# A lighter float64-to-float32 conversion of the weights, with its first pass tied to the exponentials and the Relus

## The chip, the cores and the metric

The kernel runs on one NeuronCore of a Trainium2 chip. The metric is device time in microseconds (us), the median of several executions. The names of the engines are those of the profile: PE is TensorE (matmuls; PEld its weight loads), DVE is VectorE, ACT is ScalarE, POOL is GpSimd, SP is SyncE, which here only issues DMAs.

## The reference

Inputs: q, k, v of 8 batches x 8 heads x 576 positions x 64 in float32; U (576x32), V (32x576), w_ch1 (512x2048) and w_ch2 (2048x512) in float64.

```
scores = q k^T / 8, masked: heads 0-3 the last 32 positions, heads 4-7 positions with the same pos % 32
x  = softmax(scores) v                       # 8 x 576 x 512, heads side by side
u  = x + (x^T U V)^T                         # mixing over positions, rank 32
out = u + relu(u w_ch1) w_ch2                # float32
```

The result has float32 accuracy. Each float32 operand of a large product is therefore split into a high and a low part (hi + lo, in the matmul's reduced float32 format), and each product is done in three matmuls: hi hi, hi lo, lo hi.

## The kernel before

**The main loop.** The 4608 rows of u are cut into 18 blocks of 256. A step is one block and one of 16 slices of 128 of the hidden layer: `gemm1` (12 matmuls of 256 columns into the PSUM tile `ph`, which has two buffers), then on ACT the Relu `gh` (L629), on DVE the remainder `gl` (L630, which reads `ph` and so frees it), and two steps later `gemm2` (12 matmuls of 512 columns, two tiles of 6, into an accumulator). There are 288 steps. The first two blocks run interleaved, since every slice of the weights is converted while they run.

**The attention.** Batch 0 comes ahead of the first step, batch 1 partly beside the last part of batch 0 and partly beside the first steps, and the others in windows of later steps. Batches 0 and 1 do all heads on PE; from batch 2 on the strided heads are done with products on POOL and sums on DVE (`strided_heads`). In batches 0 and 1 a pair of heads goes through: transposes of k and q on PE (L203), copies on ACT (`kZ`, `qT`), scores (L299), maximum and subtraction on DVE (L322, L324), the exponential on ACT (L325), transposes (L330), the product with v (L340), the division (L367 to L369). The mixing follows (L475 to L509), and then u^T is built (`uh`, `ul`, L590 to L595).

**The conversion of the weights.** There are 32 chunks of 128x512 (`raw`, 64-bit), in four groups of 8, 4 for `gemm1` and 4 for `gemm2`. `to_f32` makes float32 of the 64-bit patterns:

- on ACT, the absolute value of the high words read as float32 (L115);
- the maximum of this and 2^-15 (L116), by `CMODE` on POOL in six chunks of eight and on DVE in two;
- on DVE, a shift left by 3 and a mask (L118), then sign and top exponent bit or-ed in from the high words (L120), then the top 3 bits of the low words (L122);
- afterwards in `weights`, on ACT the high part (L169), and on POOL the low part, a subtraction (L170).

The three small arrays (U and two pieces of V) go through the same `to_f32`, with the maximum on DVE. All of the conversion lies ahead of about 193 us.

**What sets the order.** Each engine runs its instructions in one queue, in order. A conversion is called from the first attention's loop (one chunk in five turns) and from the step loop (by `CONVM`, and at the latest when a step needs it). The order that results on each engine is not the order of the code: a scheduler with its own estimate of times moves instructions within what the data allows. `tc.issue_after(ins)` adds to an instruction the condition that it stands behind `ins` on the same engine; before, only the weights' DMAs use it.

Of the kernel before, what the change touches and what calls it, by code (L numbers as in the profile page):

```python
# [16 lines left out]
TINY = 2.0 ** -15  # L17
# [11 lines left out]
CMODE = (1, 1, 1, 0, 1, 1, 1, 0)  # L29
# [17 lines left out]
def fused_kernel(ctx, tc, q, k, v, U, V, w1_in, w2_in, masks, eye, out):  # L47
# [31 lines left out]
    def psx2():  # L79
        """Two PSUM banks; those of the output sums serve too before the first of them."""  # L80
# [10 lines left out]
    last_dma = [None]  # L91
# [14 lines left out]
    def to_f32(raw, p, n, eng=nc.vector, one=False):  # L106
        """float32 of float64 bits: the top 24 significant bits; below float32's range 0."""
# [4 lines left out]
        if one:  # L112
            eng.tensor_scalar(out=f, in0=hi_w.bitcast(F32), scalar1=TINY, scalar2=None, op0=ALU.abs_max)
        else:
            nc.scalar.activation(out=f, in_=hi_w.bitcast(F32), func=AF.Abs)  # L115
            eng.tensor_scalar(out=f, in0=f, scalar1=TINY, scalar2=None, op0=ALU.max)  # L116
        i = cv.bitcast(I32)[0:p, 0:n]
        nc.vector.tensor_scalar(out=i, in0=i, scalar1=3, scalar2=0x3FFFFFF8,  # L118
                                op0=ALU.logical_shift_left, op1=ALU.bitwise_and)
        nc.vector.scalar_tensor_tensor(out=i, in0=hi_w, scalar=-0x40000000, in1=i,  # L120
# [39 lines left out]
    def weights():  # L160
        for n, (i, g, t) in enumerate(chunks):
# [3 lines left out]
            f = to_f32(raws[i, g, t], 128, 512, *((nc.vector, False), (nc.gpsimd, False), (nc.vector, True), (nc.gpsimd, True))[CMODE[n % 8]])  # L165
# [32 lines left out]
    def transpose_natural(dsts, xn, strided, engines):  # L198
        """dst[d, position] per head of load_natural, the positions class by class when strided."""
# [35 lines left out]
    def acquire(names):  # L235
        """The first of these buffers that no other part of the program is filling or reading, when one is free."""
        while True:
            for name in names:
                if name not in held:
                    held[name] = True  # L240
                    return name
            yield

    def value_tiles():
        """Values of two heads, each in its half of the rows and of the columns; what stays is written once."""
# [6 lines left out]
    def attention_pair(b, pr, sd, od, last):  # L252
        """Two heads of a batch: 32 positions attend to themselves and to the 32 before, in the order of the
        positions (local heads) or class by class (strided heads)."""
# [70 lines left out]
        nc.scalar.activation(out=s_sb, in_=s_sb, func=AF.Exp, scale=0.125 if early else 1.0)  # L325
# [459 lines left out]
```

## Time and profile before

| | us |
|---|---|
| median of 3 runs | 1016.41 (1016.31 to 1018.74) |
| the profiled execution: its span, the only time that the page gives of it | 1016.9 |
| PE busy | 958.7 |
| DVE busy | 648.8 |
| POOL busy | 406.1 |
| ACT busy | 313.0 |

An engine's busy time says little on its own here. The program has a first part of some 90 us, in which batch 0's attention leaves PE idle for much of the time, a second part of about 100 us, in which the steps have begun and the conversion still runs, and a third part of more than 800 us in which PE is nearly always busy. What a change to the conversion is worth is to be read from the first two parts.

### The profile page before, as it was taken

What the parts mean: (1) busy time and instruction counts of PE and PEld (TensorE: products, weight loads), DVE (VectorE), ACT (ScalarE), POOL (GpSimd) and SP (SyncE); (2) the same over time, 40 slices, a digit from 0 to 9 for tenths busy, and PEclk for the clock granted to TensorE, in tenths of its full rate; (3) what the DMA queues carried; (4) which work ended last, traced back from release to release, by engine and by line L of the source; (5) the groups of instructions that cost most, each with busy time, mean ns of one, the idle gap of its engine ahead of it and who ended that gap; (6) DMA issues with size and microseconds to landing.
All of it is one profiled execution on the core that took longest, in us unless ns stands there. A gap on an engine that the chain in (4) does not pass through costs nothing.

```text
span 1016.9 us, 18249 instructions
## 1 busy us (share of the span) xinstructions
PE 958.7 (94%) x7164; PEld 832.6 (82%) x7164; DVE 648.8 (64%) x1184; ACT 313.0 (31%) x691; POOL 406.1 (40%) x397
## 2 busy tenths in 40 slices
PE   4576889999999999999999999999999999999997
PEld 2345678898898889978889888988898889999996
DVE  3567998979786868634768686968686864312121
ACT  6777545213311241111422133123321242111110
POOL 1324966965383429201447353735383410000000
PEclk9797999999999999999999999999999999999999
DMA  7865913042523250401252425052514200101000
GB/s 189 221 164 143 366 39 67 2 109 48 91 42 68 48 90 22 88 1 42 47 91 43 68 47 91 21 89 48 91 39 71 47 22 21 42 1 43 1 21 21
DMA packets 186094, 71.33 MB, mean 70 GB/s; under 512 B 148952, under 2 KB 177272, under 8 KB 186008
## 3 DMA queue, kind: packets, MB, share of 16 engines
q1 hardware_dynamic: 186008, 70.16, 32.4%
q8 instruction: 56, 0.92, 0.4%
q14 instruction: 30, 0.25, 0.1%
HBM read 51.64 MB, written 11.80 MB: 62 GB/s over the span
## 4 chain that ended last, share of the span: by engine, by line
PE 76%; DVE 7%; SPq 5%; POOL 4%; issue 3%; DMA 3%; ACT 2%; DVEq 0%; POOLq 0%; ACTq 0%
PE ph L625 35%; PE acc L642 33%; SPq L94 4%; POOL tmp L409 3%; PE px L299 2%; PE px L340 1%; DVE cv L120 1%; DVE st L439 1%; PE px L330 1%; POOL w L170 1%; SPq L157 1%; DVE cv L122 1%; PE px L475 1%; DMA raw<-in_moe_w_ch_dram 1%; PE px L501 1%
## 5 line engine op out<-in xcount | busy, mean ns | idle before, releaser
L625 PE MATMUL ph<-uh,w 128*128 128x256 f32 x2304 | 472.6, 286 | 8.1 <-DVE gl L630 7.3
L625 PEld LDWEIGHTS ph<-uh,w 128*128 128x128 f32 x2304 | 379.3, 190 | 29.4 <-DVE gl L630 11.9
L642 PE MATMUL acc<-w,gh 128*128 128x512 f32 x1088 | 341.5, 393 | 0.0
L625 PE MATMUL ph<-ul,w 128*128 128x256 f32 x1152 | 331.5, 288 | 1.6 <-DVE ul L595 1.6
L630 DVE SCALAR_TENSOR_TENSOR gl<-ph,gh 128x256 fp32r<-128x256 f32 x288 | 120.6, 419 | 244.9 <-ACT gh L629 243.5
L629 ACT ACTIVATE gh<-ph 128x256 fp32r<-128x256 f32 x288 | 110.3, 384 | 504.9 <-PE ph L625 452.8
L437 POOL TENSOR_TENSOR tmp<-st,s_st 128x448 f32<-128x448 f32 (+7 forms) x162 | 144.2, 912 | 237.2 <-DVE st L439 148.7
L625 PEld LDWEIGHTS ph<-ul,w 128*128 128x128 f32 x1152 | 217.3, 189 | 11.4 <-DVE ul L595 1.8
L642 PEld LDWEIGHTS acc<-w,gh 128*128 128x128 f32 x1088 | 194.3, 188 | 31.2 <-issue 2.2
L642 PE MATMUL acc<-w,gl 128*128 128x512 f32 x544 | 213.2, 392 | 0.2 <-DVE gl L630 0.2
L409 POOL TENSOR_TENSOR tmp<-st 128x576 f32<-128x576 f32 (+6 forms) x162 | 169.4, 1089 | 74.9 <-DMA st<-in_k_dram 29.2
L439 DVE TENSOR_REDUCE st<-tmp 128x64 f32<-128x64 f32 (+8 forms) x162 | 138.3, 873 | 4.4 <-POOL tmp L437 3.4
L642 PEld LDWEIGHTS acc<-w,gl 128*128 128x128 f32 x544 | 102.2, 188 | 19.3 <-issue 1.1
L411 DVE TENSOR_REDUCE s_st<-tmp 128x9 f32<-128x576 f32 (+6 forms) x162 | 87.8, 564 | 14.2 <-POOL tmp L409 13.6
L170 POOL TENSOR_TENSOR w<-cv,w 128x512 fp32r<-128x512 f32 x32 | 45.3, 1424 | 49.1 <-ACT w L169 46.9
L116 POOL TENSOR_SCALAR cv<-cv 128x512 f32<-128x512 f32 x24 | 40.0, 1670 | 42.2 <-ACT cv L115 36.8
L454 ACT COPY xg<-st 32x256 f32<-32x256 f32 x96 | 38.7, 404 | 37.3 <-DVE st L439 36.4
L299 PE MATMUL px<-kZ,qT 128*32 128x128 f32 x612 | 30.5, 303 | 8.5 <-ACT qT L226 8.4
L299 PEld LDWEIGHTS px<-kZ,qT 128*32 128x32 f32 x612 | 20.4, 120 | 18.3 <-ACT qT L226 9.9
L169 ACT CAST w<-cv 128x512 fp32r<-128x512 f32 x32 | 19.7, 618 | 44.0 <-DVE cv L122 37.4
L612 DVE TENSOR_TENSOR ul<-u,uh 128x1024 fp32r<-128x1024 f32 x15 | 21.9, 1460 | 14.3 <-ACT uh L611 14.3
L120 DVE SCALAR_TENSOR_TENSOR cv<-raw,cv 128x512 int32<-128x512 int32 x32 | 28.3, 888 | 0.4
(123 smaller groups left out, 686.6 us busy)
## 6 DMA issues: line engine op xcount, KB each, us to landing
raw<-in_moe_w_ch_dram SPq DMA_DIRECT2D x32, 512.0 KB, 8.0
out_dram<-xg SPq DMA_DIRECT2D x32, 256.0 KB, 2.2
u<-bt SPq DMA_DIRECT2D x240, 32.0 KB, 1.9
vt_kept<-in_v_dram SPq DMA_DIRECT2D x28, 144.0 KB, 3.6
st<-in_q_dram SPq DMA_DIRECT2D x24, 144.0 KB, 3.4
st<-in_k_dram SPq DMA_DIRECT2D x24, 144.0 KB, 4.8
st<-in_v_dram SPq DMA_DIRECT2D x24, 144.0 KB, 3.2
xn<-in_k_dram SPq DMA_DIRECT2D x48, 72.0 KB, 2.4
```

Source lines behind the costliest of these rows:

```text
L94: last_dma[0] = nc.sync.dma_start(out=out, in_=in_).ins
L116: eng.tensor_scalar(out=f, in0=f, scalar1=TINY, scalar2=None, op0=ALU.max)
L170: nc.gpsimd.tensor_tensor(out=lo, in0=f, in1=hi.bitcast(F32), op=ALU.subtract)
L299: nc.tensor.matmul(sp[32 * c4:32 * c4 + 32, t], qT[:, 32 * c:32 * c + 32], kZ[:, :, 32 * c:32 * c + 64], start=not early, stop=True, skip_ ...
L409: nc.gpsimd.tensor_tensor(out=tmp[:, 0:n], in0=sk[:, j0:j0 + n], in1=sq[:, i:i + 1].broadcast_to([128, n, D]), op=ALU.mult)
L411: late.append(lambda tmp=tmp, n=n, i=i, j0=j0: nc.vector.tensor_reduce(out=s_st[:, i, j0:j0 + n], in_=tmp[:, 0:n], axis=AX.X, op=ALU.add))
L437: nc.gpsimd.tensor_tensor(out=tv, in0=sv[:, 0:i + 1, d0:d0 + step], in1=s_st[:, i, 0:i + 1].broadcast_to([128, i + 1, step]), op=ALU.mult)
L439: late.append(lambda tv=tv, i=i, d0=d0, step=step: nc.vector.tensor_reduce(out=o_st[:, i, d0:d0 + step], in_=tv.rearrange("p j d -> p d j" ...
L625: nc.tensor.matmul(ph[:, 0:W], w_parts[0, g, dc][:, part, fs], ut[:, :, :, dc, :], start=(dc == 0 and i == 0), stop=(dc == NDC - 1 and i = ...
L629: nc.scalar.activation(out=gh[:, 0:W], in_=ph[:, 0:W], func=AF.Relu)
L630: nc.vector.scalar_tensor_tensor(out=gl[:, 0:W], in0=ph[:, 0:W], scalar=0.0, in1=gh[:, 0:W].bitcast(F32), op0=ALU.max, op1=ALU.subtract)
L642: nc.tensor.matmul(accs[n][:, s, :], gt[:, cs], w_parts[1, g, f][:, part, :], start=(fc == 0 and i == 0), stop=(fc == NFC - 1 and i == 2))
```

## The change

`to_f32` loses the maximum altogether, on POOL as on DVE, and with it `CMODE` and `TINY`. The absolute value on ACT now multiplies by 2^-112, which moves the exponent so that the DVE shift needs no mask after it; the second DVE pass takes one bit (the sign) from the high words instead of two. The chunks of weights (not the three small arrays) get a condition on their ACT pass: it stands behind the exponential of batch 0 that the program wrote last, or, in the steps, behind the Relu it wrote last.

```diff
-    def to_f32(raw, p, n, eng=nc.vector, one=False):
+    def to_f32(raw, p, n, paced=False):
...
-        if one:
-            eng.tensor_scalar(out=f, in0=hi_w.bitcast(F32), scalar1=TINY, scalar2=None, op0=ALU.abs_max)
-        else:
-            nc.scalar.activation(out=f, in_=hi_w.bitcast(F32), func=AF.Abs)
-            eng.tensor_scalar(out=f, in0=f, scalar1=TINY, scalar2=None, op0=ALU.max)
+        with tc.issue_after(gate[0]) if paced and gate else nullcontext():
+            nc.scalar.activation(out=f, in_=hi_w.bitcast(F32), func=AF.Abs, scale=2.0 ** -112)
         i = cv.bitcast(I32)[0:p, 0:n]
-        nc.vector.tensor_scalar(out=i, in0=i, scalar1=3, scalar2=0x3FFFFFF8,
-                                op0=ALU.logical_shift_left, op1=ALU.bitwise_and)
-        nc.vector.scalar_tensor_tensor(out=i, in0=hi_w, scalar=-0x40000000, in1=i,
+        nc.vector.tensor_scalar(out=i, in0=i, scalar1=3, scalar2=None, op0=ALU.logical_shift_left)
+        nc.vector.scalar_tensor_tensor(out=i, in0=hi_w, scalar=-0x80000000, in1=i,
                                        op0=ALU.bitwise_and, op1=ALU.bitwise_or)
...
-            f = to_f32(raws[i, g, t], 128, 512, *((nc.vector, False), (nc.gpsimd, False), (nc.vector, True), (nc.gpsimd, True))[CMODE[n % 8]])
+            f = to_f32(raws[i, g, t], 128, 512, True)
...
-        nc.scalar.activation(out=s_sb, in_=s_sb, func=AF.Exp, scale=0.125 if early else 1.0)
+        exped = nc.scalar.activation(out=s_sb, in_=s_sb, func=AF.Exp, scale=0.125 if early else 1.0)
+        if b == 0:
+            gate[:] = [exped.ins]
...
-        nc.scalar.activation(out=gh[:, 0:W], in_=ph[:, 0:W], func=AF.Relu)
+        gate[:] = [nc.scalar.activation(out=gh[:, 0:W], in_=ph[:, 0:W], func=AF.Relu).ins]
```

The lines of the changed kernel have other numbers: the conversion's L115, L118, L120, L122, L169 and L170 are now L112, L114, L115, L117, L164 and L165, and L590 to L595, L629 and L630 are L587 to L592, L626 and L627.

**ACT, the last exponential of batch 0.** The queue of ACT before, around the exponential of batch 0's last pair (s_sb_492); kZ_80 is filled here for the first pair of batch 1.

```order
L226 COPY PT_446<-px_440 128x640
L115 ACTIVATE cv_495<-raw0_0_3_381 128x512
L169 CAST w0_0_3_501<-cv_495 128x512
L325 ACTIVATE s_sb_492<-s_sb_492 128x640
L226 COPY kZ_80<-px_527 64x288 x4
L226 COPY PT_549<-px_543 128x640
```

The same place now (s_sb_486).

```order
L221 COPY PT_440<-px_434 128x640
L112 ACTIVATE cv_489<-raw0_0_3_376 128x512
L164 CAST w0_0_3_494<-cv_489 128x512
L221 COPY kZ_80<-px_520 64x288 x4
L320 ACTIVATE s_sb_486<-s_sb_486 128x640
L221 COPY PT_542<-px_536 128x640
```

The four copies for batch 1 have moved ahead of the exponential.

**DVE, where the first u^T is finished.** The queue of DVE before, from the first to the second half of the first `ul`; cv_888 is the conversion of a chunk, s_sb and o_sb belong to pairs of heads of batch 1.

```order
L595 TENSOR_TENSOR ul_823<-px_824,uh_822 128x4x4x32
L118 TENSOR_SCALAR cv_888<-cv_888 128x512
L368 RECIPROCAL rt_897<-rt_897 128x8
L322 TENSOR_REDUCE mx_935<-acc_872 128x10
L120 SCALAR_TENSOR_TENSOR cv_888<-raw1_0_3_601,cv_888 128x512
L369 TENSOR_TENSOR o_sb_898<-px_845,rt_897 128x512
L367 TENSOR_SCALAR rt_897<-px_845 64x2
L324 TENSOR_TENSOR s_sb_934<-acc_872,mx_935 128x640
L595 TENSOR_TENSOR ul_823<-px_824,uh_822 128x4x4x32
```

The same place now.

```order
L592 TENSOR_TENSOR ul_813<-px_814,uh_812 128x4x4x32
L117 SCALAR_TENSOR_TENSOR cv_878<-raw1_0_3_593,cv_878 128x512
L366 TENSOR_TENSOR o_sb_887<-px_835,rt_886 128x512
L364 TENSOR_SCALAR rt_886<-px_835 64x2
L317 TENSOR_REDUCE mx_924<-acc_862 128x10
L365 RECIPROCAL rt_886<-rt_886 64x2
L592 TENSOR_TENSOR ul_813<-px_814,uh_812 128x4x4x32
L319 TENSOR_TENSOR s_sb_923<-acc_862,mx_924 128x640
```

Two passes of the conversion (shift, first or) and the subtraction of the softmax no longer stand between the halves of `ul`; the last pass of the same chunk does.

**ACT, third to fourth step.** The queue of ACT before, from the third Relu to the fourth.

```order
L629 ACTIVATE gh_1052<-ph_1039 128x256
L169 CAST w0_1_1_1002<-cv_996 128x512
L594 CAST uh_923<-px_925 128x4x4x32
L115 ACTIVATE cv_1114<-raw1_1_1_979 128x512
L115 ACTIVATE cv_1152<-raw1_1_2_981 128x512
L169 CAST w0_1_3_1070<-cv_1064 128x512
L629 ACTIVATE gh_1102<-ph_1089 128x256
```

The same place now.

```order
L626 ACTIVATE gh_1038<-ph_1025 128x256
L112 ACTIVATE cv_1050<-raw0_1_3_851 128x512
L112 ACTIVATE cv_1058<-raw1_1_0_947 128x512
L221 COPY qT_903<-acc_936 64x288
L591 CAST uh_912<-px_914 128x4x4x32
L164 CAST w0_1_0_981<-cv_976 128x512
L164 CAST w0_1_1_989<-cv_984 128x512
L164 CAST w0_1_2_1022<-cv_1017 128x512
L164 CAST w0_1_3_1055<-cv_1050 128x512
L164 CAST w1_1_0_1063<-cv_1058 128x512
L626 ACTIVATE gh_1086<-ph_1073 128x256
```

Five casts of finished chunks now stand together ahead of the fourth Relu, where two stood before.

## Rows read from the trace of the kernel before

**Rows 1.** Stretches: length, PE PEld DVE ACT POOL busy, PEclk, DMA share, GB/s.

```profile
0.00:90.00 90.00, 50.82 (x625) 35.83 (x625) 45.40 (x98) 66.73 (x107) 22.02 (x23) 0.85 0.74 185
90.00:140.00 50.00, 39.57 (x265) 32.85 (x264) 47.16 (x69) 26.81 (x51) 40.94 (x27) 0.97 0.56 217
140.00:190.00 50.00, 48.65 (x381) 41.76 (x380) 45.43 (x84) 20.73 (x44) 34.98 (x28) 1.00 0.29 54
...
240.00:1016.00 776.00, 770.28 (x5558) 677.65 (x5556) 468.13 (x859) 189.32 (x468) 272.25 (x285) 1.00 0.27 49
```

**Rows 2.** Waits of PE from 90 to 140 us: total us, times, longest.

```profile
PE ph L625 <- DVE gl L630: 5.0, 5, 1.5
PE acc L203 <- issue: 2.5, 1, 2.5
PE ph L625 <- DVE ul L595: 1.6, 1, 1.6
```

**Rows 3.** Groups by line, 90 to 140 us: busy us, mean ns; idle before, releaser.

```profile
L116 POOL TENSOR_SCALAR cv<-cv 128x512 f32<-128x512 f32 x12 | 21.3, 1787 | 5.8 <-ACT cv L115 5.8
L170 POOL TENSOR_TENSOR w<-cv,w 128x512 fp32r<-128x512 f32 x14 | 20.4, 1475 | 10.0 <-ACT w L169 10.0
L120 DVE SCALAR_TENSOR_TENSOR cv<-raw,cv 128x512 int32<-128x512 int32 x14 | 14.6, 1047 | 0.0
L118 DVE TENSOR_SCALAR cv<-cv 128x512 int32<-128x512 int32 x14 | 13.1, 948 | 0.0
L122 DVE SCALAR_TENSOR_TENSOR cv<-raw,cv 128x512 int32<-128x512 int32 x13 | 10.2, 796 | 0.0
L116 DVE TENSOR_SCALAR cv<-cv 128x512 f32<-128x512 f32 x3 | 2.7, 895 | 0.2 <-ACT cv L115 0.2
```

**Rows 4.** Single lines, whole trace: duration ns min/median/max, first and last start.

```profile
L118 DVE TENSOR_SCALAR cv<-cv x35: 176/427/1516, 18.6 to 183.9; 128x512 int32<-128x512 int32 x32, 128x160 int32<-128x160 int32 x1, 32x512 int32<-32x512 int32 x1, 32x64 int32<-32x64 int32 x1
L120 DVE SCALAR_TENSOR_TENSOR cv<-raw,cv x32: 670/692/1783, 29.3 to 185.6; 128x512 int32<-128x512 int32 x32
L122 DVE SCALAR_TENSOR_TENSOR cv<-raw,cv x32: 672/691/1782, 30.0 to 187.0; 128x512 int32<-128x512 int32 x32
L115 ACT ACTIVATE cv<-raw x32: 652/668/706, 26.5 to 176.5; 128x512 f32<-128x512 f32 x32
L325 ACT ACTIVATE s_sb<-s_sb x20: 736/740/745, 23.0 to 815.7; 128x640 f32<-128x640 f32 x20
```

**Rows 5.** Timeline of DVE, 84 to 130 us.

```profile
89.46 1.51 DVE L118 TENSOR_SCALAR cv<-cv 128x512 int32<-128x512 int32 x1
...
93.79 0.67 DVE L595 TENSOR_TENSOR ul<-px,uh 128x512 fp32r<-128x512 f32 x1
...
106.64 1.51 DVE L118 TENSOR_SCALAR cv<-cv 128x512 int32<-128x512 int32 x1
108.07 1.77 DVE L120 SCALAR_TENSOR_TENSOR cv<-raw,cv 128x512 int32<-128x512 int32 x1
...
118.50 0.68 DVE L122 SCALAR_TENSOR_TENSOR cv<-raw,cv 128x512 int32<-128x512 int32 x1
```

**Rows 6.** Timeline of POOL, 100 to 120 us: start, length, instruction, count.

```profile
106.22 3.08 POOL L170 TENSOR_TENSOR w<-cv,w 128x512 fp32r<-128x512 f32 x2
...
117.50 3.62 POOL L116 TENSOR_SCALAR cv<-cv 128x512 f32<-128x512 f32 x2
```

**Rows 7.** The head of the page.

```profile
span 1016.9 us, 18249 instructions
```

**Rows 8.** Timeline of ACT at the first Relu; in brackets the idle time before.

```profile
98.14 0.38 ACT L629 ACTIVATE gh<-ph 128x256 fp32r<-128x256 f32 x1 [0.75 <-PE ph L625]
```

**Rows 9.** The chain that ended last: start, us, what.

```profile
45.66 0.42 ACT kZ L226
...
235.18 1.45 PE ph L625 x12
```

**Rows 10.** Timeline of PE at the first step.

```profile
90.94 0.50 PE L625 MATMUL ph<-uh,w 128*128 128x256 f32 x2 [0.68 <-ACT uh L594]
```

More of the change, by code (lines that the diff above doesn't have):

```diff
@@ L1 @@
-from contextlib import ExitStack
+from contextlib import ExitStack, nullcontext
 import concourse.bass as bass
@@ L16 @@
 NEG = -1.0e9
-TINY = 2.0 ** -15
 ATT_BUFS = 7
@@ L28 @@
 PTS = 'vaaaaaaa'
-CMODE = (1, 1, 1, 0, 1, 1, 1, 0)
 W0, W1 = 2, 29
@@ L89, in psx1 @@
         return psx2()[:, 0, :]
-    last_dma = [None]
+    last_dma, gate = [None], []
     def dma(out, in_):
```

## The prediction

> **What bounds the kernel now.** First the stretches [rows 1]: from 240 us on PE is busy for 770.28 of 776.00 us. What is done there is the same matmuls before and after, so the end moves only with the time at which PE gets there. In the first 90 us PE is busy for 50.82 us, but ACT for 66.73: transposes, softmax and loads of batch 0 hand on to each other, and no single engine is full. From 90 to 140 us PE is busy for 39.57 us and DVE for 47.16 of 50, and POOL for 40.94. From 140 to 190 us PE is back at 48.65. So the place to look at is 90 to 140 us, where PE is idle for 50 - 39.57 = 10.4 us and DVE is nearly full.
>
> Second, who ended PE's waits there [rows 2]. Half of the idle time, 5.0 us in five waits, is `gemm1` waiting for `gl`: `gl` frees the PSUM tile `ph`, of which there are two, and stands on DVE between passes of the conversion. 1.6 us is a wait for `ul`, DVE's too. In 2.5 us PE stands at a transpose (L203) into a PSUM tile that DVE was still reading. POOL ends none of PE's waits. DVE sets the pace here.
>
> Third, what DVE spends there [rows 3], against what the same passes take at their median over the whole trace [rows 4]. The shift L118 takes 13.1 us for 14, at 0.427 it would be 6.0. L120 takes 14.6 us for 14, at 0.692 it would be 9.7. L122 takes 10.2 us for 13, at 0.691 it would be 9.0. Of 37.9 us these three lines lose 7.1 + 4.9 + 1.2 = 13.2 us to something. The timelines say to what: the shift at 106.64 us took 1.51 us and L120 at 108.07 took 1.77 [rows 5], both beside the two subtractions that POOL ran from 106.22 to 109.30 [rows 6]. L122 at 118.50 us took its plain 0.68 us [rows 5] while POOL was within two maxima, 117.50 to 121.12 [rows 6]. It is POOL's subtraction L170, with two inputs, that holds DVE up, and the change keeps all of these.
>
> **The change part by part.** The sum is made against the profiled execution. The page gives its span, 1016.9 us [rows 7], and no other time of it; the median of the runs is 0.5 us below that, so I take the differences from the trace and set them against 1016.4 us.
>
> The maximum on DVE. Three passes in the decisive stretch, 2.7 us [rows 3], go, and nothing takes their place. Since DVE is the engine that PE waits for there, I count them whole: -2.7 us.
>
> The maximum on POOL. Twelve passes and 21.3 us of POOL go there [rows 3]. PE waits for POOL nowhere [rows 2], so the time itself is worth nothing. It is worth what it did to DVE, a part of the 13.2 us. The lower end is nothing, by the pass at 118.50 us. The upper end is a share by POOL's busy time, 21.3 of 21.3 + 20.4 us [rows 3], which is 6.7 us. The rows that I can look at one by one stand for the lower end, but not every pass beside a maximum need be as lucky: I take 2.0 us, so -2.0.
>
> The Trainium skill, "Advanced Engine Details and Errata", section "VectorE Performance Modes", says that the second SBUF port of VectorE is shared with GpSimd, and that GpSimd's instructions and two-port Vector instructions block each other, whatever GpSimd's instruction is. By that rule the maxima would have to be charged like the subtractions, and the term would be 6.7 us rather than 2.0. The pass at 118.50 us, with two inputs in SBUF, does not bear it out; the ones beside the subtractions do.
>
> The passes that stay. The shift loses its mask, and its kind and size remain: 0.427 us [rows 4], the same again. A pass of this kind with one operation instead of two is not shown for integers; between half of that and the 0.69 of a two-input pass it would be a matter of 14 times 0.2 us, -3 to +4 us. The nearest row is the shift itself, and I take 0. The absolute value now carries a scale: 0.668 us for 512 columns without one, and the exponential, which has a scale of 0.125, 0.740 us for 640 [rows 4]. Per column that is no more; 0, at most 0.1 us each, off the path since ACT is busy for 26.81 of 50 us.
>
> The order at the first step. Before, two conversion passes and the softmax's subtraction stood on DVE between the halves of the first `ul`, the first of them 1.51 us long; the second half came at 93.79 us [rows 5]. Now one pass stands there, and the second half is nearer by up to the length of the shift, of a 0.69 us pass and of the subtraction, less the pass that takes their place. The transposes at which PE stood for 2.5 us [rows 2] come behind most of the first two `gemm1` in the new order of PE. The ends are 0 and -2.5 us. What is put off on DVE is still to be done, but from 140 us on the conversion runs without holding PE up, so a part is kept: -1.0.
>
> The condition on the absolute value. At the first step the Relu was not held by one: it waited 0.75 us for PE [rows 8]. One absolute value ahead of a Relu would be 0.67 us, but DVE, not ACT, is late, and I take 0.
>
> Batch 0. The four copies `kZ` that have moved ahead of its last exponential take 0.42 us each [rows 9]; uncovered, that is +1.7 us on a chain that reaches the first step. Against it stands a maximum on DVE that this chain no longer holds, 0.4 us if it is like the shift [rows 4]. The ends are -0.4 and +1.7. The exponential also waits for the subtraction behind three conversion passes of the chunk, which hides most of the copies: +0.2.
>
> After 140 us. PE is idle for 1.35 us up to 190 us, and for 5.7 us after 240 [rows 1]; small changes of order may move either by a microsecond, to both sides: 0.
>
> Sum: -2.7 - 2.0 - 1.0 + 0.2 = -5.5, and 1016.4 - 5.5 = 1010.9 us.
>
> **The rivals.**
>
> POOL's maximum held DVE up as the subtraction does. For it: POOL is busy for 40.94 of 50 us there, half of it with maxima, and the passes are slow on the mean. Against it: the pass at 118.50. The price: -2.7 - 6.7 - 1.0 + 0.2 = -10.2, and 1006.2 us. (It is the rule of the Trainium skill cited above, taken at its word.) More than the idle time of 10.4 us and the 1.35 us behind it cannot be had after 90 us; that would be 1004.6.
>
> The subtractions take back what the maximum gives. POOL is free earlier, each subtraction starts as soon as its cast is done, when DVE is in the passes of the next chunk, and more of them hit. Each of the 14 subtractions in the stretch cost 13.2 / 14 = 0.94 us on the mean; three more hits eat the 2.7 us, and no contention goes. What is left is -1.0 + 0.2: 1015.6 us. For it: all that is slow in the rows looked at lies beside L170. Against it: the 14 subtractions cost that much already, so most must hit now.
>
> The slower side: five casts ahead of the fourth Relu on ACT. They wait for the last passes of five chunks, and by the new order DVE has twelve instructions between the third and the fourth `gl`: two shifts, three L120, five L122, a copy and a half of `ul`. At their medians the ten passes take 2 x 0.427 + 3 x 0.692 + 5 x 0.691 = 6.4 us, at their longest 2 x 1.516 + 3 x 1.783 + 5 x 1.782 = 17.3 [rows 4], 10.9 more. PE has two `gemm1` of 1.45 us [rows 9] to do in the meantime, and both buffers of `ph` are then full; 10.9 - 2.9 = 8.0 us would be lost. With the rest of the sum without the order's 1.0 (-2.7 - 2.0 + 0.2) that ends at 1016.4 + 8.0 - 4.5 = 1019.9 us. It decides from the point where more than half of the ten passes are held up. For it: the casts are followed by their subtractions on POOL. Against it: those subtractions come after the casts, when most of the ten passes are through.
>
> **How the numbers follow.** Forecast 0.53, with a range of its own from 1008.5 to 1013.4; POOL's maximum as a blocker 0.17; taken back by the subtractions 0.20; the late Relu 0.10. The range reaches from 1004.5, all idle time gone, to 1017.0, the second rival with the copies `kZ` uncovered; below it I leave 0.04 and above it 0.10. A measurement here can tell a difference of about 0.3%, 3 us, from none: faster means under 1013.4, slower over 1019.4. Faster: 0.50 of the 0.53, the 0.17 and a little of the second rival, 0.68. Slower: most of the last rival, 0.08. The same: 0.24.
>
> **What would show it.** Between 90 and 140 us of the changed kernel the shift, L120 and L122 should lose some 11 us to POOL instead of 13.2, the long ones all beside the subtraction; PE's waits for `gl` should fall from 5.0 us to about 2, and the wait of 2.5 us at the transposes should go. The first `gemm1` should begin within 1.5 us of 90.94 us [rows 10]. If its start has moved by more, the reading of batch 0 is wrong. If the three lines come to their medians, the first rival is right; if PE still waits 5 us for `gl` the second; and one wait of over 4 us at the fourth or fifth `gemm1` would be the third. A start-up of steady steps that is earlier by 5 us, and an end that is not, would mean that the time was given back after 240 us, which I hold to be excluded.

## The result: slightly slower, and the profile after

The changed kernel takes 1021.21 us (median of 15 runs, 1018.84 to 1023.35), the kernel before 1019.11 beside it (15 runs): a ratio of 1.0025 [1.0014, 1.0036], or 2.5 us slower, where 5.5 us faster were forecast. The time lies outside the range, and so does the ratio. Two of the three runs of before that stood ahead of the prediction were low ones: beside the experiments its medians lay between 1018.4 and 1019.75 us. (A run's time is some 1.8 us above the span of its profile in all runs here, so the profiled execution of before, with its span of 1016.9 us, was one of about 1018.7 us.) So everything below goes by ratios; times 1019 us they give the differences in us.

The stretches of the changed kernel, with the columns of [rows 1]:

```profile
0.00:90.00 90.00, 54.66 (x597) 38.96 (x601) 41.84 (x91) 66.11 (x106) 12.29 (x16) 0.72 0.72 182
90.00:140.00 50.00, 40.23 (x288) 34.17 (x280) 40.76 (x68) 26.05 (x51) 21.04 (x14) 0.93 0.59 223
...
240.00:1016.00 776.00, 773.44 (x5575) 680.16 (x5573) 467.76 (x859) 189.26 (x470) 271.05 (x285) 1.00 0.27 49
```

From 90 to 140 us DVE is busy for 6.4 us less than before (40.76 for 47.16) and POOL for half as long, and PE is no better served: 40.23 us for 39.57, at a granted clock of 0.93 for 0.97. The relief arrived and bought nothing. What the passes of the conversion take in that stretch, against [rows 3]:

```profile
L165 POOL TENSOR_TENSOR w<-cv,w 128x512 fp32r<-128x512 f32 x13 | 20.0, 1551 | 34.7 <-ACT w L164 30.3 <-DMA raw<-in_moe_w_ch_dram 4.3
L117 DVE SCALAR_TENSOR_TENSOR cv<-raw,cv 128x512 int32<-128x512 int32 x14 | 11.7, 845 | 0.0
L115 DVE SCALAR_TENSOR_TENSOR cv<-raw,cv 128x512 int32<-128x512 int32 x14 | 11.5, 838 | 0.0
L114 DVE TENSOR_SCALAR cv<-cv 128x512 int32<-128x512 int32 x14 | 9.7, 708 | 2.7 <-ACT cv L112 2.6
```

Against the medians of [rows 4] (0.427, 0.692, 0.691) the 14 of each lose 3.9 + 2.0 + 2.2 = 8.1 us, not the 13.6 of before nor the 11 forecast. (Here and below a loss is counted from the rows' mean times. The prediction's 13.2 is counted from their busy times; from the means the same rows give 7.3 + 5.0 + 1.4 = 13.6.) PE's waits in the same stretch are others than in [rows 2]:

```profile
PE ph L622 <- ACT uh L591: 4.8, 2, 3.3
PE acc L639 <- DVE qT L223: 2.9, 1, 2.9
PE px L587 <- DVE ul L592: 0.9, 1, 0.9
PE px L639 <- ACT gh L626: 0.5, 1, 0.5
PE px L498 <- DVE ul L592: 0.4, 1, 0.4
PE acc L639 <- ACT gh L626: 0.2, 1, 0.2
```

The 5.0 us for `gl` are gone and so are the 2.5 at the transposes. In their place stand two waits that before did not have: 4.8 us for the cast `uh` and 2.9 us for a copy of `qT`. Where they come from is read on timelines (start, length; in brackets the idle time before and its releaser). PE before, at the transposes:

```profile
93.97 0.83 PE L203 MATMUL acc<-ident,xn 128*128 128x128 f32 x5 [2.52 <-issue]
```

The changed kernel, PE:

```profile
94.07 0.51 PE L622 MATMUL ph<-uh,w 128*128 128x256 f32 x2 [1.53 <-ACT uh L591]
...
99.89 0.55 PE L198 MATMUL acc<-ident,xn 128*128 128x128 f32 x3
...
107.08 0.50 PE L622 MATMUL ph<-uh,w 128*128 128x256 f32 x2 [3.31 <-ACT uh L591]
...
111.82 0.70 PE L639 MATMUL acc<-w,gh 128*128 128x512 f32 x2 [2.91 <-DVE qT L223]
```

ACT:

```profile
98.17 0.38 ACT L626 ACTIVATE gh<-ph 128x256 fp32r<-128x256 f32 x1 [1.78 <-PE ph L622]
100.00 1.71 ACT L221 COPY kZ<-px 64x288 f32<-64x288 f32 x4 [1.45 <-PE px L198]
...
102.21 0.42 ACT L221 COPY qT<-acc 64x288 f32<-64x288 f32 x1
102.52 1.25 ACT L112 ACTIVATE cv<-raw 128x512 f32<-128x512 f32 x2
...
106.44 0.58 ACT L591 CAST uh<-px 128x512 fp32r<-128x512 f32 x1
...
119.11 0.38 ACT L626 ACTIVATE gh<-ph 128x256 fp32r<-128x256 f32 x1 [3.00 <-PE ph L622]
119.39 0.66 ACT L112 ACTIVATE cv<-raw 128x512 f32<-128x512 f32 x1
```

DVE:

```profile
98.58 0.42 DVE L627 SCALAR_TENSOR_TENSOR gl<-ph,gh 128x256 fp32r<-128x256 f32 x1 [1.47 <-ACT gh L626]
102.35 0.69 DVE L592 TENSOR_TENSOR ul<-px,uh 128x512 fp32r<-128x512 f32 x1 [3.34 <-ACT uh L591]
...
108.00 1.51 DVE L114 TENSOR_SCALAR cv<-cv 128x512 int32<-128x512 int32 x1
109.43 1.75 DVE L115 SCALAR_TENSOR_TENSOR cv<-raw,cv 128x512 int32<-128x512 int32 x1
111.21 0.46 DVE L223 COPY qT<-acc 64x288 f32<-64x288 f32 x1
...
119.53 0.43 DVE L627 SCALAR_TENSOR_TENSOR gl<-ph,gh 128x256 fp32r<-128x256 f32 x1 [4.12 <-ACT gh L626]
```

The five transposes into `acc` that stood at 93.97 us before now come at 99.89 us (three) and 100.72 us (two). On ACT the copy `qT` that needs them, at 102.21 us, stands ahead of the absolute values of the ninth and tenth chunk, which therefore start at 102.52 us; before, these two started at 95.19 us. DVE has no pass to do and stands idle 1.47 and 3.34 us. It then pays in the wrong place: from 108 us two passes are drawn out to 1.51 and 1.75 us, behind them the copy of `qT` is late, the PSUM tile `acc` is not free, and the first `gemm2` starts at 111.82 us; the fourth Relu, at 119.11, has waited 3.00 us for PE. The absolute value of the 14th chunk stands behind this Relu on ACT and starts at 119.39 us (107.89 before); DVE has no pass left and is idle for another 4.12 us. The three idle times, 8.9 us, are nearly all of DVE's 9.2 in the stretch. The first Relu is where it was (98.17 us for 98.14 in [rows 8]), although the first `gemm1` is 3.1 us later than in [rows 10].

### The profile page after: what moved, and what is told of

The parts are those of the page before. It is cut to its first block, busy times and chain, and to the rows that moved or that the text cites. A ratio compares the mean times of both kernels' runs of the same rounds, so it can differ in the third digit from the quotient of the medians.

```text
span 1020.9 us, 18211 instructions
## 1 busy us (share of the span) xinstructions
PE 965.3 (95%) x7164; PEld 838.4 (82%) x7164; DVE 634.4 (62%) x1173; ACT 312.6 (31%) x691; POOL 365.9 (36%) x373
## 4 chain that ended last, share of the span: by engine, by line
PE 80%; DVE 9%; ACT 3%; DMA 3%; SPq 2%; issue 2%; POOL 0%; DVEq 0%; ACTq 0%; POOLq 0%
PE ph L622 37%; PE acc L639 34%; SPq L92 2%; PE px L294 2%; PE px L337 2%; DVE cv L115 1%; DMA xn<-in_q_dram 1%; DVE cv L117 1%; PE px L639 1%; DVE cv L114 1%; DVE st L436 1%; ACT qT L221 1%; PE px L472 1%; DVE gl L627 1%; PE px L327 1%
## 5 line engine op out<-in xcount | busy, mean ns | idle before, releaser
L627 DVE SCALAR_TENSOR_TENSOR gl<-ph,gh 128x256 fp32r<-128x256 f32 x288 | 120.6, 419 | 248.6 <-ACT gh L626 247.4
L626 ACT ACTIVATE gh<-ph 128x256 fp32r<-128x256 f32 x288 | 110.4, 383 | 519.8 <-PE ph L622 474.0
L165 POOL TENSOR_TENSOR w<-cv,w 128x512 fp32r<-128x512 f32 x32 | 45.8, 1441 | 128.0 <-ACT w L164 123.5
L114 DVE TENSOR_SCALAR cv<-cv 128x512 int32<-128x512 int32 (+3 forms) x35 | 20.4, 592 | 19.4 <-ACT cv L112 19.3
L164 ACT CAST w<-cv 128x512 fp32r<-128x512 f32 x32 | 19.6, 617 | 31.9 <-DVE cv L117 31.2
L117 DVE SCALAR_TENSOR_TENSOR cv<-raw,cv 128x512 int32<-128x512 int32 x32 | 26.5, 835 | 0.3
```

The source lines that it names most:

```text
L117: nc.vector.scalar_tensor_tensor(out=i, in0=lo_w, scalar=29, in1=i, op0=ALU.logical_shift_right, op1=ALU.bitwise_or)
L165: nc.gpsimd.tensor_tensor(out=lo, in0=f, in1=hi.bitcast(F32), op=ALU.subtract)
L626: gate[:] = [nc.scalar.activation(out=gh[:, 0:W], in_=ph[:, 0:W], func=AF.Relu).ins]
L627: nc.vector.scalar_tensor_tensor(out=gl[:, 0:W], in0=ph[:, 0:W], scalar=0.0, in1=gh[:, 0:W].bitcast(F32), op0=ALU.max, op1=ALU.subtract)
```

## The experiments

The condition on the absolute value is called the gate here. In light_free and heavy_gate the scheduler orders the queues, as in the two kernels compared. In all others each queue is written out by an explicit order of its instructions (`pin` in the diffs), so that nothing moves but what the edit says. after_q_first, which moves one load alone, takes the changed kernel's time (+2.0 and +2.5 us), so writing the queues out changes little there; the kernel before was not run in its own order written out. The brackets are 95% intervals; in microseconds they reach 1 to 2 to either side.

| kernel | median us | ratio to before | us |
|---|---|---|---|
| changed kernel | 1021.21 | 1.0025 [1.0014, 1.0036] | +2.5 |
| light_before_order | 1014.01 | 0.9954 [0.9938, 0.9969] | -4.7 |
| light_free | 1027.79 | 1.0087 [1.0070, 1.0104] | +8.9 |
| heavy_gate | 1018.67 | 0.9988 [0.9973, 1.0002] | -1.2 |
| after_q_first | 1020.67 | 1.0020 [1.0008, 1.0033] | +2.0 |
| after_both_early | 1019.16 | 1.0012 [0.9998, 1.0027] | +1.2 |
| after_qT_early | 1019.28 | 1.0009 [0.9996, 1.0023] | +0.9 |
| after_uh_early | 1023.59 | 1.0057 [1.0042, 1.0071] | +5.8 |
| heavy_after_order | 1045.41 | 1.0269 [1.0251, 1.0287] | +27.4 |
| after_tr_early | 1019.51 | 1.0010 [1.0001, 1.0020] | +1.0 |
| after_tr_uh_early | 1020.17 | 1.0015 [1.0004, 1.0026] | +1.5 |
| no_pool_max | 1014.31 | 0.9961 [0.9945, 0.9977] | -4.0 |
| no_dve_max | 1017.37 | 0.9989 [0.9978, 1.0001] | -1.1 |
| one_input_low | 1009.18 | 0.9914 [0.9899, 0.9928] | -8.8 |
| light_low_on_dve | 1011.45 | 0.9908 [0.9890, 0.9927] | -9.4 |
| old_to_relu1 | 1020.32 | 1.0006 [0.9992, 1.0020] | +0.6 |
| old_to_relu6 | 1018.31 | 0.9995 [0.9983, 1.0008] | -0.5 |
| old_to_relu13 | 1016.93 | 0.9967 [0.9950, 0.9983] | -3.4 |
| new_to_relu1 | 1017.67 | 0.9967 [0.9953, 0.9982] | -3.4 |

**The change taken apart: conversion, gate, order.** The lighter conversion without the gate, in the order of before less its 35 maxima (light_before_order, below also the light kernel in the old order):

```diff
-        with tc.issue_after(gate[0]) if paced and gate else nullcontext():
-            nc.scalar.activation(out=f, in_=hi_w.bitcast(F32), func=AF.Abs, scale=2.0 ** -112)
+        nc.scalar.activation(out=f, in_=hi_w.bitcast(F32), func=AF.Abs, scale=2.0 ** -112)
...
+    pin(tc, nc, ORDER_OF_BEFORE_WITHOUT_MAXIMA)
```

> The lighter conversion without the condition, every engine's queue pinned to the order of the kernel before with the 35 maxima taken out. Theory (the order lost what the conversion gave): 4 to 7 us faster than before, 1012 to 1015 us where before has 1019, with PE's waits for gl in the first steps well under 5 us. Rival A (the subtractions take back what the maxima gave): within 2 us of before. Rival B (the lighter passes are slower in themselves, or PE's clock falls when it has less to do early on): as the changed kernel, 2 us slower than before.

It measured -4.7 us, as expected. The same code with its order left to the scheduler (light_free, the last line of the diff absent):

> The lighter conversion without the condition on the absolute value; the scheduler orders freely. Theory: the scheduler moves the same load of q behind the gather of batch 0's strided heads as in the changed kernel, so the mixing of batch 0 starts late again and most of the gain of 4 to 7 us is lost: within 3 us of before. Rival (the condition is what costs): 4 to 7 us faster than before.

It measured +8.9 us, outside both expectations: the same instructions, 13.6 us apart by the scheduler's order and what follows from it. From 90 to 140 us PE waits 6.2 us for `gl` there, and the granted clock is 0.80 against 0.90 in light_before_order; how much of the 13.6 us each of them is worth was not tried. The conversion of before with the gate of the change (heavy_gate):

```diff
+            with tc.issue_after(gate[0]) if paced and gate else nullcontext():
+                nc.scalar.activation(out=f, in_=hi_w.bitcast(F32), func=AF.Abs)
-            nc.scalar.activation(out=f, in_=hi_w.bitcast(F32), func=AF.Abs)
             eng.tensor_scalar(out=f, in0=f, scalar1=TINY, scalar2=None, op0=ALU.max)
...
```

> The conversion of the kernel before, with its maxima, and the condition on the absolute value. Theory (the condition is worth little by itself, the load of q stays ahead of the gather): within 2 us of before. Rival (the condition costs): 2 us slower or more, as the changed kernel.

The gate alone gives -1.2 us with an interval that reaches to nothing; with the lighter passes it takes 8.9 - 2.5 = 6.4 us off. So in the order of before the light conversion is worth what it was priced at, and the order that comes with it takes more than that away. The fourth (after_q_first), a transfer of batch 0 put earlier in the changed kernel's queue of SP:

```diff
+SP  xn <- q          (the load of the next pair's queries)
 SP  xg <- od         (the gather)
-SP  xn <- q
```

> The changed kernel with every queue pinned to its own order, except that SP issues the load of q for the second pair of batch 1 ahead of the gather of batch 0's strided heads, as the kernel before does. Theory: the copy that opens the mixing of batch 0 no longer waits behind the copies of that q; it comes 3 to 5 us earlier than the 72.9 us of the changed kernel, and the end 2 to 4 us earlier than the changed kernel's. Rival (the time was lost at the first steps, not here, and anything won ahead of them is lost there): the end moves by less than 1 us.

+2.0 us, the changed kernel's time. The copy that opens the mixing comes at 72.98 us instead of 72.87: it doesn't wait for this load, and my reading falls. Nothing was won ahead of the first steps, so the run says nothing on the rival.

**The waits of the first steps, undone one by one.** In the changed kernel's queues, rows moved up (`both`; `qT` and `uh` move the rows so named alone):

```diff
 ACT  gh (second Relu)
+ACT  qT (second copy)
 ACT  gh (third Relu)
+ACT  uh (second cast)
 ACT  cv cv cv (absolute values)
-ACT  qT
-ACT  uh
 DVE  gl (second)
+DVE  qT (second copy)
 DVE  gl (third)
+DVE  ul (second half)
...
-DVE  qT
-DVE  ul
```

> The changed kernel with every queue kept as it is, but for four rows of the first steps: on ScalarE the second copy of qT goes right behind the second Relu and the second cast of uh right behind the third, ahead of three absolute values; on VectorE the second copy of qT goes right behind the second gl and the second half of ul behind the third, ahead of seven conversion passes. Theory (the loss of about 7 us at the fourth Relu comes from these four standing behind passes that the subtractions on GpSimd draw out): the waits of 3.3 us for uh and 2.9 us for the copy of qT go, the first gemm2 begins near 108 us instead of 111.82, the fourth Relu comes 4 to 6 us before 119.11, and the time falls by 4 to 6 us, to 1015 to 1017. Rival (VectorE is full there in any order, so that what is put behind comes late in its place): other waits of together over 4 us appear before the sixth Relu, and the time stays within 2 us of the changed kernel's.

> As the one before, with the two copies of qT moved alone. Theory: the output sum's PSUM tile comes free by 106 us, but TensorE still stands 3.3 us for uh at the fourth gemm1; the wait of 2.9 us ahead of gemm2 goes, and the time falls by 2 to 3 us, to about 1018.5. Rival (it is the late cast of uh alone): no change, within 1 us of the changed kernel.

> As the first, with the second cast of uh and the second half of ul moved alone. Theory: the fourth gemm1 goes on at about 105.3 us instead of 107.08, but gemm2 still waits for the copy of qT, which stays at about 111 us: at most 1 us is won. Rival (the late cast is what counts): 3 us or more are won.

With both, the first `gemm2` starts at 107.22 us instead of 111.82 and the fourth Relu at 114.51 instead of 119.11, as expected; the time moves by -1.3 us where 4 to 6 were expected. `qT` alone gives -1.6 (2 to 3 expected), `uh` alone +3.3, which neither theory had. The profile of after_uh_early, of the fastest of its five runs, doesn't show where the 3.3 us lie: its Relus come up to 1.3 us ahead of the changed kernel's. With both moved PE still waits 3.7 us for `uh`, 2.2 for `gh` and 2.0 for `gl` up to 140 us, as the rival of after_both_early has it. The next step up, the late transposes themselves and all that hangs on them (after_tr_early; without the gate, since the two absolute values move ahead of what it ties them to):

```diff
 PE   ph <- uh (first two matmuls of gemm1)
+PE   acc <- xn  x5
...
-PE   acc <- xn  x5
 ACT  s_sb (exponential)
+ACT  qT, cv, cv, qT
...
 DVE  s_sb
+DVE  qT
 DVE  xg xg
+DVE  qT, cv (shift)
 DVE  gl (first)
+DVE  cv (second pass), cv (shift)
...
```

> The queues of the changed kernel, but the five transposes of the next pair's queries (PSUM tile acc_936) stand on TensorE behind the first two matmuls of gemm1, as before the change, and with them what can only follow them: both pairs of copies of qT on ScalarE and VectorE, two absolute values, and two shifts and one pass behind them. Theory (putting the transposes off was the loss: the buffers of cv are given out behind qT, so the conversion stops, and VectorE stood idle 1.5 and 3.3 us up to 102.35 us): these two idle times of VectorE go, the first gemm2 begins before 106 us instead of 111.82, the fourth Relu comes 4 to 6 us before 119.11, and the time falls by 4 to 6 us, to 1015 to 1017. Rival (the two idle times were slack, and the rest of the order is what costs): within 2 us of the changed kernel.

> As the one before, and the second cast of uh and the second half of ul go right behind the third Relu and the third gl too, ahead of conversion passes. Theory: it adds 1 to 2 us to the gain of the transposes, since TensorE stood 3.3 us for this cast; about 1014 to 1016, what the lighter conversion gave in the old order (1014.0). Rival: nothing is added, within 1 us of the run with the transposes alone.

With the transposes early the fourth Relu comes at 113.77 us, where the light kernel in the old order has it (113.78), and the 2.9 us for `qT` are gone. PE's waits between 90 and 140 us there:

```profile
PE ph L622 <- ACT uh L591: 2.9, 2, 1.5
PE px L639 <- ACT gh L626: 1.6, 1, 1.6
PE px L587 <- DVE ul L592: 1.5, 2, 0.9
PE acc L198 <- issue: 1.1, 1, 1.1
PE ph L622 <- DVE gl L627: 1.0, 2, 0.5
```

But the time falls by 1.5 us only, and `uh` adds nothing. My theory was right about the mechanism of these waits and wrong about their worth: the rival, that the rest of the order costs, holds for most of it. The Relus show where: the eighth comes at 125.60 us (123.29 in light_before_order) and the twelfth at 144.03 (138.73).

**Where the order loses.** The same light conversion, with the order of before up to one Relu and the changed kernel's for all that is left, or the reverse:

```diff
-    pin(tc, nc, ORDER_OF_BEFORE_WITHOUT_MAXIMA)
+    pin(tc, nc, THAT_ORDER_UP_TO_RELU_K + REST_IN_ORDER_OF_THE_CHANGED_KERNEL)
```

> The lighter conversion, with the queues of before up to the first Relu and the changed kernel's order of all that is left behind it. Theory A (the loss lies in the first twelve steps, 98 to 142 us): it keeps the loss, 1019 to 1021 us. Theory B (the loss lies in batch 0: what was left undone at the first Relu, and TensorE's half clock there): 1014 to 1016. Theory C (it lies behind 142 us): 1018 to 1021.

> The lighter conversion, with the queues of before up to the sixth Relu (about 117 us) and the changed kernel's order of what is left. Theory (the loss of the first twelve steps lies at the first five, where the profile of the changed kernel shows its waits): 1015.5 to 1017.5, ratio 0.996 to 0.998. Rival (it lies at the sixth to twelfth step, by work that was put off): 1019 to 1020.5, as with the splice at the first Relu.

> As the one before, with the queues of before up to the thirteenth Relu (about 145 us). Theories A and B: the loss is gone, 1013.5 to 1016. Theory C (it lies behind 142 us): 1018 to 1021.

> The reverse: the lighter conversion, with the changed kernel's order up to the first Relu and the order of before for all that is left behind it. Theories A and C: little is lost in batch 0, 1014 to 1016. Theory B: the loss is kept, 1018 to 1021.

From the light kernel (-4.7) to the changed one (+2.5) are 7.2 us. Each part below is a difference of two kernels and uncertain by about 2 us, so the 4.0 alone is well clear of noise. Batch 0 has 1.3 of them by one pair (-4.7, -3.4) and 1.9 by the other (+0.6, +2.5). The steps from the first Relu to the thirteenth have 4.0 (+0.6, -3.4): 1.1 in the first five, 2.9 in those behind (-0.5, -3.4). What lies behind the thirteenth Relu has 1.3 (-3.4, -4.7). So theory A holds for more than half, and of its steps perhaps rather the later ones; batch 0 and the rest share what is left. In microseconds old_to_relu6 (1018.31), old_to_relu13 (1016.93) and new_to_relu1 (1017.67) all fell between the ranges expected for them: no theory holds alone. In the stretch from 116 to 150 us the light kernel in the old order shows one wait of PE and this row of the stretch:

```profile
PE ph L622 <- DVE gl L627: 0.9, 2, 0.5
116.00:150.00 34.00, 32.91 (x264) 28.39 (x263) 31.89 (x51) 16.16 (x34) 15.79 (x12) 1.00 0.41 138
```

and the one that changes over at the sixth Relu:

```profile
PE ph L622 <- DVE gl L627: 2.3, 3, 1.4
PE px L639 <- ACT gh L626: 1.3, 1, 1.3
116.00:150.00 34.00, 30.32 (x241) 24.89 (x240) 32.88 (x49) 15.77 (x32) 17.12 (x12) 1.00 0.35 126
```

PE loses 2.6 us of work there (32.91 to 30.32), to `gl` between drawn-out passes again and to a `gemm2` that comes so close behind its own Relu that it waits for it. after_tr_early, with the first steps mended, has nearly the same two waits in this stretch, 2.4 and 1.3 us. A candidate is the conversion's place on ACT: there too the 14th absolute value stands behind the fourth Relu, at 114.04 us, where light_before_order has it at 106.33. Which rows do it was not tried.

**Both orders with the heavy passes.** The kernel heavy_gate in the changed kernel's queues, each maximum right ahead of the instruction that it stood ahead of:

```diff
+    pin(tc, nc, ORDER_OF_THE_CHANGED_KERNEL_WITH_THE_MAXIMA)
```

> The conversion of before (mask in the shift, a maximum behind each absolute value) in the queues of the changed kernel, the 35 maxima right ahead of the instruction that they stood ahead of. Theory (order and conversion add up): slower than the changed kernel by the 4.6 us that the lighter conversion gave in the order of before, to about 1025.5. Rival (the lighter conversion is worth little in this order, since what holds TensorE there is the order): within 2 us of the changed kernel.

Both expectations fall: heavy_after_order takes +27.4 us, 24.9 above the changed kernel. PE waits for `gl` 12.0 us between 90 and 190 us there:

```profile
PE ph L628 <- DVE gl L633: 12.0, 6, 4.5
```

These are about half of the 24.9 us. Order and conversion don't add up: this order, drawn up for short passes, was very sensitive to long ones. So the prices -4.7 (conversion) and +7.2 us (order) hold for the way that takes the conversion first; the other way round they would be +27.4 for the order and -24.9 for the conversion.

**What POOL costs DVE.** Two kernels in the order of before, no_pool_max and no_dve_max, each without one kind of maximum (the diff is the first's; the second has `is not`):

```diff
-            eng.tensor_scalar(out=f, in0=f, scalar1=TINY, scalar2=None, op0=ALU.max)
+            if eng is nc.vector:
+                eng.tensor_scalar(out=f, in0=f, scalar1=TINY, scalar2=None, op0=ALU.max)
```

> The kernel before with its queues kept, and without the 24 maxima on GpSimd (the lower bound of 2^-15 is left out in these chunks); the 11 on VectorE and the rest of the conversion stay. My sum gave the maxima on VectorE 2.7 us and those on GpSimd 2.0 of the 4.6 that the lighter conversion measured. Theory: 1.5 to 2.5 us faster than before, about 1016.5. Rival (GpSimd's maximum held VectorE up as its subtraction does): 3.5 us or more, and the maxima on VectorE are worth little. Second rival (one-input work on GpSimd holds nothing up): 0 to 1 us.

> The kernel before with its queues kept, and without the 11 maxima on VectorE (the lower bound of 2^-15 is left out in these chunks); the 24 on GpSimd stay. By the sum of the prediction 2.7 us are won, about 1016; by the difference of the two measurements (4.6 for all without, 4.0 for GpSimd's) 0.6 us, within the noise of before.

GpSimd's 24 maxima are worth 4.0 us [2.3, 5.6], as the first rival has it, though the interval reaches into the theory's range; VectorE's 11 are worth 1.1 us [-0.1, 2.2], which leaves out the 2.7 of the sum. The rows of no_pool_max, 90 to 140 us:

```profile
L119 DVE TENSOR_SCALAR cv<-cv 128x512 int32<-128x512 int32 x15 | 12.0, 809 | 0.0
L121 DVE SCALAR_TENSOR_TENSOR cv<-raw,cv 128x512 int32<-128x512 int32 x15 | 11.9, 801 | 0.1
L123 DVE SCALAR_TENSOR_TENSOR cv<-raw,cv 128x512 int32<-128x512 int32 x14 | 10.1, 735 | 0.1
```

Over the medians they lose 5.7 + 1.6 + 0.6 = 8.0 us (rounded parts), 5.6 less than the 13.6 of before. light_before_order, without POOL's maxima too, loses 10.5 (below), 3.1 less. So the one-input maximum did some 3 to 6 us to DVE in this stretch. The trace of before had shown it, in rows beside those of [rows 5] and [rows 6]:

```profile
100.68 1.66 POOL L116 TENSOR_SCALAR cv<-cv 128x512 f32<-128x512 f32 x1
100.92 1.09 DVE L122 SCALAR_TENSOR_TENSOR cv<-raw,cv 128x512 int32<-128x512 int32 x1
...
119.70 0.83 DVE L118 TENSOR_SCALAR cv<-cv 128x512 int32<-128x512 int32 x1
```

The shift at 119.70 us lies beside the same two maxima as the pass at 118.50 us, and takes twice its median. Then the subtraction, in the light kernel with the order of before (one_input_low, which therefore computes something else):

```diff
-            nc.gpsimd.tensor_tensor(out=lo, in0=f, in1=hi.bitcast(F32), op=ALU.subtract)
+            nc.gpsimd.tensor_scalar(out=lo, in0=hi.bitcast(F32), scalar1=2.0 ** -15, scalar2=None, op0=ALU.max)
```

> The lighter conversion in the queues of before (1014.0 us), with GpSimd's subtraction of the two inputs f and hi replaced by a maximum of hi with 2^-15, which has one input: the low part of a weight is not computed. It waits for the same cast. Theory (only the two-input instruction holds VectorE up): between 90 and 140 us the shift and the two passes behind it come to their medians of 0.43, 0.69 and 0.69 us, VectorE loses under 3 us there instead of some 11, and the time falls by 3 to 8 us, to 1006 to 1011. Rival (any instruction of GpSimd blocks VectorE, or the second operand's traffic is not what counts): the passes stay as long as they are, and the time is within 2 us of 1014.

and, with the subtraction as it was but of 23 chunks on VectorE (light_low_on_dve),

```diff
-            nc.gpsimd.tensor_tensor(out=lo, in0=f, in1=hi.bitcast(F32), op=ALU.subtract)
+            (nc.vector if 7 <= n < 30 else nc.gpsimd).tensor_tensor(out=lo, in0=f, in1=hi.bitcast(F32), op=ALU.subtract)
```

> The lighter conversion in the queues of before (1014.0), with the subtractions of 23 chunks (the eighth to the thirtieth) on VectorE at the places in the order that they had on GpSimd. The run with a one-input instruction in their place won 4.8 us. Theory (a subtraction costs VectorE 0.69 us of its own and takes away 0.94 us of holding up): 14 x 0.25 = 3 us faster at most, 1011 to 1014. Rival (VectorE now stands at each subtraction for ScalarE's cast): 1015 or more.

The rows of 90 to 140 us, of the light kernel with the subtraction on POOL:

```profile
L165 POOL TENSOR_TENSOR w<-cv,w 128x512 fp32r<-128x512 f32 x15 | 22.0, 1480 | 36.6 <-ACT w L164 30.8 <-issue 5.7
L117 DVE SCALAR_TENSOR_TENSOR cv<-raw,cv 128x512 int32<-128x512 int32 x15 | 13.3, 899 | 0.1
L114 DVE TENSOR_SCALAR cv<-cv 128x512 int32<-128x512 int32 x15 | 12.0, 810 | 0.0
L115 DVE SCALAR_TENSOR_TENSOR cv<-raw,cv 128x512 int32<-128x512 int32 x15 | 12.0, 802 | 0.1
```

with one input in its place:

```profile
L165 POOL TENSOR_SCALAR w<-w 128x512 fp32r<-128x512 f32 x16 | 26.2, 1646 | 27.9 <-ACT w L164 22.2 <-issue 5.7
L117 DVE SCALAR_TENSOR_TENSOR cv<-raw,cv 128x512 int32<-128x512 int32 x16 | 12.2, 774 | 0.1
L115 DVE SCALAR_TENSOR_TENSOR cv<-raw,cv 128x512 int32<-128x512 int32 x16 | 11.8, 741 | 0.1
...
L114 DVE TENSOR_SCALAR cv<-cv 128x512 int32<-128x512 int32 x16 | 9.4, 599 | 0.0
```

and with the subtraction on DVE:

```profile
L115 DVE SCALAR_TENSOR_TENSOR cv<-raw,cv 128x512 int32<-128x512 int32 x16 | 11.0, 690 | 0.1
L165 DVE TENSOR_TENSOR w<-cv,w 128x512 fp32r<-128x512 f32 x15 | 10.2, 684 | 0.3 <-ACT w L164 0.3
L117 DVE SCALAR_TENSOR_TENSOR cv<-raw,cv 128x512 int32<-128x512 int32 x15 | 10.1, 683 | 0.0
...
L114 DVE TENSOR_SCALAR cv<-cv 128x512 int32<-128x512 int32 x16 | 7.7, 488 | 0.0
```

The three passes lose 5.7 + 1.7 + 3.1 = 10.5 us beside 15 subtractions, 0.70 us each; 2.8 + 0.8 + 1.3 = 4.9 us beside 16 one-input instructions, 0.30 each, more than half of it at the shift; and 0.8 us with a single subtraction left on POOL in the stretch. (Per subtraction the price varies with the order: 8.1 us beside 13 are 0.62 in the changed kernel.) Both theories of one_input_low were too plain: one input holds DVE up too, at under half the price. Its time, 1009.18, is in the expected range all the same.

The last kernel is the fastest here that computes the low parts, and beats both kernels compared: 1011.45 us, 0.9908 of before. (one_input_low, at 0.9914, can't be told from it.) DVE's 10.2 us for the subtractions are about what it gets back (10.5 - 0.8 = 9.7), so the 4.7 us over the light kernel are more than DVE's busy time explains; PE's waits for `gl` are down to 0.4 us there, and a chunk's low part comes after 0.68 us instead of 1.48. How the two share the gain was not tried. (The Trainium skill, "GPSIMD Engine Reference", section "Engine selection", sends elementwise work to VectorE, GpSimd being about twice as slow with two inputs. The rows agree: 0.684 against 1.480 us.)

## Why the prediction was wrong

*The step that failed* is the order: "The order at the first step", taken at -1.0, with the nothing that I put down for the rest of the new order, under "The condition on the absolute value" and "After 140 us". I took the 2.5 us that PE stood at the transposes for a loss that would go. They did go, and the work that stands behind them on ACT and DVE went late with them, which cost 4.8 us of idle DVE at the first step and 3.3 + 2.9 us of PE's. And I looked at the first step alone and took the rest of a new order to be neutral, a microsecond to either side. With the light conversion it costs 7.2 us in all: about 4 in the first twelve steps, and, not well clear of noise, 1.3 to 1.9 in batch 0 (+0.2 in the sum) and 1.3 behind the twelve steps. The first step's own transposes are worth only some 1.5. What in the later steps holds PE up stays open in its causes; the splices and the Relu times show the place.

*The condition.* I asked whether an absolute value holds up a Relu. The trace shows the reverse: the 14th absolute value starts at 119.39 us, right behind the fourth Relu, after DVE had run out of passes. What this place costs wasn't tried by itself. The gate as a whole did not cost: -1.2 us with the heavy passes, -6.4 with the light ones left to the scheduler.

*The maximum on DVE* was -2.7 and measured -1.1 us: the passes do go, but less than half of their busy time in the stretch comes back.

*The maximum on POOL* was -2.0 and measured -4.0 us. I took the term near its lower end on the word of one pass, at 118.50 us in [rows 5], that had been lucky: the shift behind it was drawn out beside the same maxima, and the rows give 3 to 6 us of DVE. The first rival was right that the maximum holds DVE up, and wrong that it does so as the subtraction does. (The Trainium skill, "Advanced Engine Details and Errata", "VectorE Performance Modes", names GpSimd's instructions without distinction where it says that they and two-port Vector instructions block each other. The runs agree that a one-input instruction holds VectorE up, and differ by kind in the size: 0.30 us for it, 0.70 for two inputs.)

*Together* the two terms were -4.7 and measured -4.7: two errors that cancel. So the conversion was priced right for the order of before, but by luck in the parts.

*The passes that stay* came out as forecast: the shift with one operation has a median of 0.421 us in the changed kernel, against 0.427 for two, and the absolute value with the scale one of 0.667 us against 0.668.

*The rivals.* The subtractions did not take the gain back (8.1 us of loss in the passes, for 13.6). The slower rival had the place nearly right, the fourth Relu, 7.0 us late; but its holder was not the five casts: that Relu waited 3.00 us for PE, behind `uh` and `qT`. That its +3.5 us came near the measured +2.5 is luck. Of those 7.0 us, 5.0 were won back by the nineteenth Relu (166 us), and 2.0 lost again behind it: in the profiled executions the end is 4.0 us late. What was won back is the lighter conversion's: against light_before_order the changed kernel is 5.3 us late at the fourth Relu and 7.4 at the nineteenth.

*The signs that I named* told a part of it: the `gl` waits are gone (about 2 us were forecast to stay) and so are the 2.5 us; the first `gemm1` is 3.1 us late, where more than 1.5 would speak against the reading of batch 0; and no single wait of PE is over 4 us, so that the late Relu's sign stayed away. None of them looked at what DVE does when it runs out of passes.

## What to carry to other kernels

A change that lets a scheduler order anew is two changes: price the order apart from the instructions, by running the new instructions in the old order and splicing the orders at a few points, since here they were worth -4.7 and +7.2 us (and, as heavy_after_order shows, don't simply add up). Before a wait is booked as a gain, follow what stands behind the waiting instruction on the other engines; a transpose that PE waited for fed two engines that had, by the order of their queues, nothing else to do. And a helper engine's price is also what it does to its neighbour: in light_before_order 0.70 us of VectorE for each 1.48 us subtraction on GpSimd.

## What the runs showed of the hardware

A fuller engine beside less contention was the faster kernel: DVE with the subtractions of its own, and POOL nearly idle, gave 1011.45 us. A one-input GpSimd instruction costs VectorE's passes 0.30 us on the mean, though single passes beside it run at their plain 0.68 us; of the 4.9 us lost beside 16 such instructions, 2.8 fall on the one-input shift.

The granted clock in the first 90 us was 0.72 in the changed kernel's profile against 0.85 in [rows 1], so TensorE ran longer at the lower of its two levels. What that cost was not tried by itself. light_low_on_dve, among the fastest, had 0.75 there. And over 120 executions of before, 10 us more at half clock (twice the missing share of the mean clock, times the span) go with 0.7 us more of time, a loose connection (correlation 0.30); the changed kernel's median is 57 us of it for 49, which by this would be half a microsecond.
